# A fused attention and two-layer feed-forward kernel: zero matmuls in TensorE's waits, a new order of the work ahead of the first gate product, and another order of weight conversion

## The chip, the cores and the metric

The kernel runs on one core of a Trainium2 chip. The metric is the device time of one execution in microseconds (us): the median of the executions that were timed. A NeuronCore has a matmul engine (TensorE; PE in the profile, with its weight loads as PEld), a vector engine (VectorE; DVE), an activation engine (ScalarE; ACT), a general one (GpSimd; POOL) and a queue that issues DMAs (SyncE; SP). Each works through its own list of instructions in order; an instruction that waits holds up everything behind it on its engine.

## The reference

Windowed attention over 4 batches, 8 heads, 768 positions of 64 (chunks of 32 queries, each with 8 memory keys, 16 positions to the left and 8 to the right), then two feed-forward stages over 3072 tokens of width 512, all in float32:

```python
scores = scale * np.matmul(q_c, k_full.transpose(0, 1, 3, 2))
a = np.exp(scores - np.max(scores, axis=-1, keepdims=True))
out[:, :, c_start:c_end] = np.matmul(a / (np.sum(a, axis=-1, keepdims=True) + 1e-09), v_full)
...
gate = 1.0 / (1.0 + np.exp(-(x @ w_gate)))          # w_gate, w_val: 512 x 1536
x = gate * (x @ w_val) @ w_out                      # w_out: 1536 x 512
...
h = x @ w_in                                        # 512 x 2048
g = (a[0] + a[1]*h + a[2]*h*h + a[3]*h**3) / (1.0 + np.abs(b[0])*np.abs(h) + np.abs(b[1])*h*h + 1e-6)
return g @ w_out
```

The weights of both stages reach the chip as float64 words (8 bytes each).

## The kernel before

**Tiles.** The attention works on 24 tiles of 128 query rows (32 queries of four chunks, all eight heads). Per tile `attn_qk` makes the scores in two PSUM banks `sp` (L98), `attn_max` takes the row maximum and subtracts it on DVE (L122, L123 or, away from the ends of a sequence, L129, L131), `attn_exp` is one ACT instruction (L137), `attn_sum` and `attn_mul` normalise on DVE (L144 to L146, L150), `attn_t` transposes on TensorE (`tp`, L157) and copies on ACT (L159), and `attn_pv` multiplies with the values (`xp`, L172) and writes the result as a pair of halves: the part that the matmul format holds, by ACT (L181), and the rest, by DVE (L182). Four tiles make one block `x` of 512 tokens.

**First feed-forward stage.** Six blocks j by twelve slices f of the hidden width are 72 steps. A step runs `gate_val` twice (m = 0 gate, m = 1 value; L250), each 12 products of 128x128 by 128x512: four pieces of the inner dimension times three terms (high by high, high by low, low by high). ACT makes the sigmoid `sg` of the gate (L259), DVE multiplies it with the value product (L262), and `g_split` makes the pair `g` of it (ACT L268, then DVE L269). `out1` of a step runs one step later: 12 products that add up in four PSUM banks `acc` (L282) over a block's twelve steps. The second stage (from L331) comes after block 5.

**Weights.** Slice f has three units of weights, (f, 0) gate, (f, 1) value, (f, 2) output. In block 0 each is loaded (`load_stage`, 512 KB, tile `st`) and converted from float64: `conv_scale`, two ACT instructions (L202, L203); `conv_mag`, then `conv_sign`, one DVE instruction each (L207, L214), which leave float32 in `wf`. Before a unit is used in any block it is split into the pair `wp`: `split_hi` on ACT (L233), `split_lo` on DVE (L237). So in block 0 a unit costs three instructions on ACT and three on DVE, and they depend on each other in the order scale, mag, sign, hi, lo.

**Order.** The order on every engine is that in which the program is written. Ahead of the 72 steps stands a list written out by hand (L488 on): loads, the attention of tiles 0 to 3, and the conversion of the six units of f = 0 and 1 and the scaling of the units of f = 2. In the steps a plan says what is done in each: split of slice f+1, bits (`bits1`: mag and sign) of f+2, scaling of f+3, parts of later attention tiles:

```python
run(w1_hi, attn_exp, bits1)
gate_val(j, f, 0, c0, n)
run(w1_lo, attn_sum, attn_mul, pv, attn_t)
gate_val(j, f, 1, c0, n)
run(scale1)
g_split((1, j, f, c0), sgs.pop((j, f, c0)), n)
run(attn_qk, attn_max, conv2)
```

A PSUM bank of the pool `ps` (four banks; `acc` holds the other four) is given out again when its last reader is through.

## Time and profile before

| | |
|---|---|
| three timed executions | 1206.11, 1207.27, 1208.91 us; median 1207.27 |
| the profiled execution | 1208.78 us, of which 1207.0 us lie between the first and the last instruction (its span) |
| busy time of PE | 1185.7 us, 98% of the span |
| busy time of DVE, ACT | 891.4 us (74%), 749.2 us (62%) |
| first score product | 4.60 us after the span's start |
| first gate product | 30.84 us |
| first output product (`acc`) | 44.76 us |

The profile gives each engine's busy time, tables of busy time and granted TensorE clock by stretch, the instructions in order of time, and for each idle stretch what ended it. Matmuls overlap, so PE counts as busy while products follow each other, whatever the clock is.

### The profile page before, as it was taken

Reading aid. Unit: us, or ns where it says so; the run is one execution under the profiler, and the core shown is the slowest. Engines: PE = TensorE matmul, PEld = TensorE weight load, DVE = VectorE, ACT = ScalarE, POOL = GpSimd, SP = SyncE. Lnnn points to the kernel's source line nnn. Section 1 sums busy time; section 2 is a strip of 40 time slices with the busy share of each in tenths; the row PEclk is TensorE's granted clock in tenths of the full one; section 3 lists DMA queues with packets and bytes.
Section 4 is the critical chain, followed back from the end, with each engine's and each line's share of the span. In section 5 each row is a group of like instructions: output and inputs, shape, how many; then the busy total and the mean of one; then the engine's idle time right before and its main releaser. Section 6 shows DMA issues by size and latency. Waiting matters only on the chain.

```text
span 1207.0 us, 19977 instructions
## 1 busy us (share of the span) xinstructions
PE 1185.7 (98%) x8064; PEld 973.7 (81%) x8064; DVE 891.4 (74%) x1458; ACT 749.2 (62%) x1302; POOL 2.1 (0%) x15
## 2 busy tenths in 40 slices
...
GB/s 366 293 189 128 24 153 57 136 89 164 80 121 154 68 111 85 169 71 74 162 150 53 36 70 9 39 23 9 53 18 1 53 18 1 52 18 1 36 1 35
DMA packets 39980, 101.69 MB, mean 84 GB/s; under 512 B 4560, under 2 KB 4560, under 8 KB 39888
## 3 DMA queue, kind: packets, MB, share of 16 engines
...
q8 instruction: 63, 1.03, 0.4%
...
## 4 chain that ended last, share of the span: by engine, by line
PE 92%; DVE 3%; ACT 2%; DMA 2%; issue 0%; SPq 0%; POOL 0%; POOLq 0%; DVEq 0%
PE h L250 29%; PE acc L370 22%; PE h L331 22%; PE acc L282 15%; PE xp L172 2%; PE sp L98 1%; PE tp L157 1%; DMA st<-w_in 1%; DMA v<-v_in 1%; DVE wf L207 1%; DVE wp L237 1%; DVE wf L214 1%; ACT st L202 0%; ACT st L203 0%; ACT g L268 0%
## 5 line engine op out<-in xcount | busy, mean ns | idle before, releaser
L250 PE MATMUL h<-x,wp 128*128 128x512 f32 x1728 | 416.0, 394 | 1.3 <-DVE wp L237 0.8
L250 PEld LDWEIGHTS h<-x,wp 128*128 128x128 f32 x1728 | 324.2, 189 | 69.7 <-DVE wp L237 1.5
L331 PE MATMUL h<-x,wp 128*128 128x512 f32 x1152 | 276.5, 389 | 0.0
L370 PE MATMUL acc<-wp,g 128*128 128x512 f32 x1152 | 275.9, 389 | 0.0
L331 PEld LDWEIGHTS h<-x,wp 128*128 128x128 f32 x1152 | 216.2, 188 | 44.9
L370 PEld LDWEIGHTS acc<-wp,g 128*128 128x128 f32 x1152 | 216.2, 188 | 44.9
L282 PE MATMUL acc<-g,wp 128*128 128x512 f32 x864 | 211.0, 393 | 0.0
L282 PEld LDWEIGHTS acc<-g,wp 128*128 128x128 f32 x864 | 160.6, 188 | 35.3
L268 ACT ACTIVATE g<-sg 128x512 fp32r<-128x512 f32 x72 | 45.5, 632 | 180.7 <-DVE sg L262 180.7
L339 ACT ACTIVATE t<-h,cf 128x512 f32<-128x512 f32 x96 | 74.7, 778 | 131.1 <-PE h L331 131.1
L262 DVE TENSOR_TENSOR sg<-sg,h 128x512 f32<-128x512 f32 x72 | 49.5, 687 | 130.8 <-PE h L250 126.7
L237 DVE TENSOR_TENSOR wp<-wf,wp 128x512 fp32r<-128x512 f32 x216 | 136.2, 684 | 0.1
L233 ACT ACTIVATE wp<-wf 128x512 fp32r<-128x512 f32 x216 | 120.9, 621 | 5.9 <-DVE c L214 4.0
L342 DVE TENSOR_TENSOR t<-t,h 128x512 f32<-128x512 f32 x96 | 65.9, 686 | 47.8 <-ACT hh L341 46.4
L259 ACT ACTIVATE sg<-h 128x512 f32<-128x512 f32 x72 | 43.0, 597 | 88.8 <-PE h L250 88.7
L269 DVE TENSOR_TENSOR g<-sg,g 128x512 fp32r<-128x512 f32 x72 | 49.9, 693 | 52.1 <-ACT g L268 52.1
L343 DVE SCALAR_TENSOR_TENSOR t<-t,cf,h 128x512 f32<-128x512 f32 x96 | 71.8, 748 | 3.4
L351 ACT ACTIVATE y<-qq,qc 128x512 f32<-128x512 f32 x96 | 70.1, 730 | 3.9 <-DVE qq L344 3.3
L357 DVE SCALAR_TENSOR_TENSOR qq<-qq,y 128x512 f32<-128x512 f32 x96 | 65.8, 686 | 8.2 <-ACT y L352 8.2
L344 DVE SCALAR_TENSOR_TENSOR qq<-hh,cab,qq 128x512 f32<-128x512 f32 x96 | 71.7, 747 | 0.0
L358 DVE SCALAR_TENSOR_TENSOR t<-t,cf,y 128x512 f32<-128x512 f32 x96 | 71.6, 746 | 0.0
L359 DVE SCALAR_TENSOR_TENSOR t<-qq,t 128x512 f32<-128x512 f32 x96 | 66.5, 693 | 3.3
...
## 6 DMA issues: line engine op xcount, KB each, us to landing
...
```

The source lines that it names most:

```text
L233: nc.scalar.activation(out=wp[key][:, 0], in_=src, func=ACTF.Copy)
L237: nc.vector.tensor_tensor(out=t[:, 1], in0=src, in1=t[:, 0].bitcast(F32), op=ALU.subtract)
L250: nc.tensor.matmul(pt, lhsT=w[:, a, kt * P : (kt + 1) * P], rhs=x[:, kt, b, c0 : c0 + n], start=(kt == 0 and i == 0), stop=(kt == KT - 1 a ...
L282: nc.tensor.matmul(acc[j][d][:, c0 : c0 + n], lhsT=w[:, a, d * P : (d + 1) * P], rhs=g[:, b, 0:n], start=(f == 0 and c0 == 0 and i == 0), ...
L331: nc.tensor.matmul(hp, lhsT=w[:, a, kt * P : (kt + 1) * P], rhs=x[:, kt, b], start=(kt == 0 and i == 0), stop=(kt == KT - 1 and i == 2),)
L339: nc.scalar.activation(out=t, in_=hp, func=ACTF.Identity, scale=cf[:, 3:4], bias=cf[:, 2:3])
L343: nc.vector.scalar_tensor_tensor(out=t, in0=t, scalar=cf[:, 1:2], in1=hp, op0=ALU.add, op1=ALU.mult)
L344: nc.vector.scalar_tensor_tensor(out=qq, in0=hh, scalar=cab[:, 1:2], in1=qq, op0=ALU.mult, op1=ALU.add)
L351: nc.scalar.activation(out=y, in_=qq, func=ACTF.Abs_reciprocal_sqrt, bias=qc[:, 0:1])
L358: nc.vector.scalar_tensor_tensor(out=t, in0=t, scalar=cf[:, 0:1], in1=y, op0=ALU.add, op1=ALU.mult)
L359: nc.vector.scalar_tensor_tensor(out=t, in0=qq, scalar=2.0, in1=t, op0=ALU.subtract, op1=ALU.mult)
L370: nc.tensor.matmul(acc[j][m], lhsT=g[:, a, m * P : (m + 1) * P], rhs=w[:, b], start=(f == 0 and i == 0), stop=(f == NF2 - 1 and i == 2),)
```

## The change

1. **Zero matmuls.** A constant tile `warm_in` of zeros (one DVE memset) and one `ps` bank. `warm(n)` issues n float32 matmuls of 128x128 by 128x256 into it; nothing reads them. 15 of them stand between the attention steps ahead of the first gate product.
2. **Scores in other banks.** The first four tiles' scores go to the `acc` banks (tiles 1 and 2 to 0 and 1, tiles 0 and 3 to 2 and 3) rather than to `ps`.
3. **Tile order.** Loads and attention of the first block go by tiles 1, 0, 2, 3. `attn_pv` is cut in two, the products and the writing of `x` (`attn_x`), which the list places apart.
4. **Weights.** The units are loaded and converted in the order (0,0), (0,1), (1,0), (1,1), (0,2), (1,2). The scaling of the three units of f = 2 and their bits, and the split of (1,2), move out of the list into step 0, behind `g_split`. In all later steps `bits1` stands behind `w1_lo` and not ahead of the gate products.

```diff
-        sps = [ps(f"sp{t}_{h}")[:, 0 : 4 * KEYS].rearrange("p (r w) -> p r w", r=4) for h in range(2)]
+        if early is None:
+            sps = [ps(f"sp{t}_{h}") for h in range(2)]
+        else:
+            sps = [accp.tile([P, 512], F32, tag=f"acc{early + h}", name=f"sp{t}_{h}") for h in range(2)]
...
+    warm_in = const.tile([P, 256], F32, name="warm_in")
+    nc.vector.memset(warm_in, 0.0)
+    warm_ps = ps("warm")
+
+    def warm(n):
+        for _ in range(n):
+            nc.tensor.matmul(warm_ps[:, 0:256], lhsT=warm_in[:, 0:P], rhs=warm_in, start=True, stop=True)
+
+    def conv1(f, m):
+        conv_mag(f"1_{f}_{m}", unit1(f, m))
+        conv_sign(f"1_{f}_{m}", unit1(f, m))
+    def hi0(f, m):
+        split_hi((1, 0, f, m), unit1(f, m))
+    def lo0(f, m):
+        split_lo((1, 0, f, m), unit1(f, m))
...
+        load_qk(1)
         load_qk(0)
-        load_qk(1)
+        load_v(1)
         load_qk(2)
-        load_v(1)
         load_v(0)
         load_qk(3)
-        load_w1(0)
+        load_v(2)
+        load_stage("1_0_0", w1[:, 0, 0:512])
         load_v(3)
+        for f, m in ((0, 1), (1, 0), (1, 1), (0, 2), (1, 2), (2, 0), (2, 1), (2, 2)):
+            load_stage(f"1_{f}_{m}", w1[:, f, m * 512 : (m + 1) * 512])
...
+        warm(5)
+        attn_qk(1, 0)
...
+        attn_t(3)
+        hi0(0, 0)
+        conv_mag("1_0_1", unit1(0, 1))
+        warm(2)
+        attn_pv(3)
+        conv_sign("1_0_1", unit1(0, 1))
+        lo0(0, 0)
+        to_x(3)
+        hi0(0, 1)
+        conv_scale("1_1_0")
+        warm(2)
+        lo0(0, 1)
+        conv1(1, 0)
+        hi0(1, 0)
+        conv_scale("1_1_1")
+        conv_mag("1_1_1", unit1(1, 1))
+        lo0(1, 0)
+        conv_sign("1_1_1", unit1(1, 1))
+        hi0(1, 1)
+        conv_scale("1_0_2")
...
-            run(w1_hi, attn_exp, bits1)
+            run(w1_hi, attn_exp)
             gate_val(j, f, 0, c0, n)
-            run(w1_lo, attn_sum, attn_mul, pv, attn_t)
+            run(w1_lo)
+            if si:
+                run(bits1)
+            run(attn_sum, attn_mul, pv, attn_t)
             gate_val(j, f, 1, c0, n)
             run(scale1)
             g_split((1, j, f, c0), sgs.pop((j, f, c0)), n)
+            if not si:
+                split_hi((1, 0, 1, 2), unit1(1, 2))
+                for m in range(3):
+                    conv_scale(f"1_2_{m}")
+                split_lo((1, 0, 1, 2), unit1(1, 2))
+                run(bits1)
```

How this stands on the engines is shown at three places. In the names, `st1_f_m` is the loaded unit (f, m), `wf` its float32 form, `wp1_0_f_m` its pair in block 0, `sg0_f` and `g1_0_f` the gate of step f and its pair; the number behind the last underscore only counts buffers.

First, ACT from the last writing of `x` to the sigmoid of step 0. Before:

```order
L202 ACTIVATE st1_1_1_125<-st1_1_1_125 128x512 [waits DMAHW0_49]
L203 ACTIVATE st1_1_1_125<-st1_1_1_125 128x512
L202 ACTIVATE st1_2_2_135<-st1_2_2_135 128x512 [waits DMAHW5_49]
L203 ACTIVATE st1_2_2_135<-st1_2_2_135 128x512
L202 ACTIVATE st1_2_0_131<-st1_2_0_131 128x512 [waits DMAHW3_49]
L203 ACTIVATE st1_2_0_131<-st1_2_0_131 128x512
L202 ACTIVATE st1_2_1_133<-st1_2_1_133 128x512 [waits DMAHW4_49]
L203 ACTIVATE st1_2_1_133<-st1_2_1_133 128x512
L233 ACTIVATE wp1_0_1_0_555<-wf1_403 128x512 [waits DVE_49]
L233 ACTIVATE wp1_0_1_1_557<-wf2_535 128x512 [waits DVE_49]
L233 ACTIVATE wp1_0_1_2_559<-wf2_535 128x512
L259 ACT_TABLE_LOAD
```

And changed:

```order
L211 ACTIVATE st1_1_0_125<-st1_1_0_125 128x512 [waits DMAHW6_49]
L212 ACTIVATE st1_1_0_125<-st1_1_0_125 128x512
L242 ACTIVATE wp1_0_1_0_541<-wf1_538 128x512 [waits DVE_49]
L211 ACTIVATE st1_1_1_127<-st1_1_1_127 128x512 [waits DMAHW7_49]
L212 ACTIVATE st1_1_1_127<-st1_1_1_127 128x512
L242 ACTIVATE wp1_0_1_1_549<-wf2_545 128x512 [waits DVE_49]
L211 ACTIVATE st1_0_2_129<-st1_0_2_129 128x512 [waits DMAHW0_49]
L212 ACTIVATE st1_0_2_129<-st1_0_2_129 128x512
L242 ACTIVATE wp1_0_0_2_556<-wf1_538 128x512 [waits DVE_49]
L211 ACTIVATE st1_1_2_131<-st1_1_2_131 128x512 [waits DMAHW1_49]
L212 ACTIVATE st1_1_2_131<-st1_1_2_131 128x512
L268 ACT_TABLE_LOAD
```

Four scalings and then three splits in a row have become an alternation of one split and one scaling, where each split waits for DVE.

Second, DVE in the same place, up to the last bits of these units. Before:

```order
L207 SCALAR_TENSOR_TENSOR wf2_535<-st1_1_1_125 128x512 [waits DMAHW0_49,Activation_49]
L207 SCALAR_TENSOR_TENSOR wf2_535<-st1_1_2_127 128x512 [waits DMAHW1_49]
L237 TENSOR_TENSOR wp1_0_0_2_489<-wf1_403,wp1_0_0_2_489 128x512
L214 SCALAR_TENSOR_TENSOR wf2_535<-st1_1_2_127,wf2_535 128x512 [waits DVE_49]
L214 SCALAR_TENSOR_TENSOR wf2_535<-st1_1_1_125,wf2_535 128x512
L207 SCALAR_TENSOR_TENSOR wf3_561<-st1_2_0_131 128x512 [waits DMAHW3_49,Activation_49]
L207 SCALAR_TENSOR_TENSOR wf3_561<-st1_2_1_133 128x512 [waits DMAHW4_49,Activation_49]
L207 SCALAR_TENSOR_TENSOR wf4_564<-st1_2_2_135 128x512 [waits DMAHW5_49]
L214 SCALAR_TENSOR_TENSOR wf3_561<-st1_2_0_131,wf3_561 128x512 [waits DVE_49]
L214 SCALAR_TENSOR_TENSOR wf3_561<-st1_2_1_133,wf3_561 128x512 [waits DVE_49]
L214 SCALAR_TENSOR_TENSOR wf4_564<-st1_2_2_135,wf4_564 128x512 [waits DVE_49]
```

And changed:

```order
L216 SCALAR_TENSOR_TENSOR wf1_538<-st1_1_0_125 128x512 [waits DMAHW6_49,Activation_49]
L223 SCALAR_TENSOR_TENSOR wf1_538<-st1_1_0_125,wf1_538 128x512 [waits DVE_49]
L216 SCALAR_TENSOR_TENSOR wf2_545<-st1_1_1_127 128x512 [waits DMAHW7_49,Activation_49]
L246 TENSOR_TENSOR wp1_0_1_0_541<-wf1_538,wp1_0_1_0_541 128x512 [waits DVE_49]
L223 SCALAR_TENSOR_TENSOR wf2_545<-st1_1_1_127,wf2_545 128x512 [waits DVE_49]
L216 SCALAR_TENSOR_TENSOR wf1_538<-st1_0_2_129 128x512 [waits DMAHW0_49,Activation_49]
L246 TENSOR_TENSOR wp1_0_1_1_549<-wf2_545,wp1_0_1_1_549 128x512 [waits DVE_49]
L223 SCALAR_TENSOR_TENSOR wf1_538<-st1_0_2_129,wf1_538 128x512 [waits DVE_49]
L216 SCALAR_TENSOR_TENSOR wf2_545<-st1_1_2_131 128x512 [waits DMAHW1_49,Activation_49]
L246 TENSOR_TENSOR wp1_0_0_2_556<-wf1_538,wp1_0_0_2_556 128x512 [waits DVE_49]
L223 SCALAR_TENSOR_TENSOR wf2_545<-st1_1_2_131,wf2_545 128x512 [waits DVE_49]
```

Two or three instructions of a kind followed each other; now each `mag` (L216) waits for ACT's scaling of its own unit, and the bits of f = 2 are no longer here.

Third, DVE from the low half of the first `g` on. Before:

```order
L269 TENSOR_TENSOR g1_0_0_0_607<-sg0_0_0_582,g1_0_0_0_607 128x512 [waits Activation_49]
L207 SCALAR_TENSOR_TENSOR wf4_564<-st1_3_0_545 128x512 [waits DMAHW6_49]
L207 SCALAR_TENSOR_TENSOR wf5_627<-st1_3_1_547 128x512 [waits DMAHW7_49]
L207 SCALAR_TENSOR_TENSOR wf5_627<-st1_3_2_549 128x512 [waits DMAHW0_49]
L214 SCALAR_TENSOR_TENSOR wf4_564<-st1_3_0_545,wf4_564 128x512 [waits DVE_49]
L214 SCALAR_TENSOR_TENSOR wf5_627<-st1_3_1_547,wf5_627 128x512 [waits DVE_49]
L214 SCALAR_TENSOR_TENSOR wf5_627<-st1_3_2_549,wf5_627 128x512 [waits DVE_49]
L237 TENSOR_TENSOR wp1_0_2_0_620<-wf3_561,wp1_0_2_0_620 128x512 [waits Activation_49]
L237 TENSOR_TENSOR wp1_0_2_1_622<-wf3_561,wp1_0_2_1_622 128x512 [waits DMAHW2_49,Activation_49]
L237 TENSOR_TENSOR wp1_0_2_2_624<-wf4_564,wp1_0_2_2_624 128x512 [waits Activation_49]
L262 TENSOR_TENSOR sg0_1_0_646<-sg0_1_0_646,h0_1_1_0_651 128x512 [waits PE_49,Activation_49]
```

And changed:

```order
L278 TENSOR_TENSOR g1_0_0_0_608<-sg0_0_0_586,g1_0_0_0_608 128x512 [waits Activation_49]
L246 TENSOR_TENSOR wp1_0_1_2_611<-wf2_545,wp1_0_1_2_611 128x512 [waits Activation_49]
L216 SCALAR_TENSOR_TENSOR wf3_620<-st1_2_0_133 128x512 [waits DMAHW2_49,Activation_49]
L216 SCALAR_TENSOR_TENSOR wf3_620<-st1_2_1_135 128x512 [waits DMAHW3_49,Activation_49]
L216 SCALAR_TENSOR_TENSOR wf4_623<-st1_2_2_137 128x512 [waits DMAHW4_49,Activation_49]
L223 SCALAR_TENSOR_TENSOR wf3_620<-st1_2_0_133,wf3_620 128x512 [waits DVE_49]
L223 SCALAR_TENSOR_TENSOR wf3_620<-st1_2_1_135,wf3_620 128x512 [waits DVE_49]
L223 SCALAR_TENSOR_TENSOR wf4_623<-st1_2_2_137,wf4_623 128x512 [waits DVE_49]
L246 TENSOR_TENSOR wp1_0_2_0_638<-wf3_620,wp1_0_2_0_638 128x512 [waits Activation_49]
L246 TENSOR_TENSOR wp1_0_2_1_640<-wf3_620,wp1_0_2_1_640 128x512 [waits Activation_49]
L246 TENSOR_TENSOR wp1_0_2_2_642<-wf4_623,wp1_0_2_2_642 128x512 [waits Activation_49]
L216 SCALAR_TENSOR_TENSOR wf4_623<-st1_3_0_563 128x512 [waits DMAHW6_49]
```

Between the low half of `g` of step 0 and the low splits of f = 2 (`wp1_0_2_m`) stood the bits of f = 3; now the low split of (1,2) and the bits of f = 2 stand there, and the bits of f = 3 come after those splits.

## Rows read from the trace of the kernel before

**Rows 1.** The page, busy time (share of the span) and instructions of each engine.

```profile
PE 1185.7 (98%) x8064; PEld 973.7 (81%) x8064; DVE 891.4 (74%) x1458; ACT 749.2 (62%) x1302; POOL 2.1 (0%) x15
```

**Rows 2.** Stretches: length, busy us (instructions) by engine, granted clock, DMA share, GB/s.

```profile
17.50:21.00 3.50, 2.08 (x71) 1.71 (x71) 3.36 (x9) 3.50 (x8) 0.00 (x0) 1.00 1.04 402
21.00:34.60 13.60, 10.68 (x205) 8.92 (x204) 10.94 (x22) 10.82 (x25) 0.00 (x0) 0.50 1.03 405
34.60:99.50 64.90, 62.58 (x574) 50.20 (x573) 57.99 (x102) 52.97 (x95) 0.34 (x2) 1.00 0.66 229
99.50:103.00 3.50, 3.50 (x10) 2.69 (x9) 3.50 (x7) 3.50 (x8) 0.00 (x0) 0.51 0.45 112
```

**Rows 3.** PE in order of time: start, us, line, tiles, count [idle before, releaser].

```profile
4.60 1.17 PE L98 MATMUL sp<-k,q 64*32 64x64 f32 x64 [4.60 <-DMA k<-k_in]
...
17.83 1.14 PE L172 MATMUL xp<-at,v 64*64 64x32 f32 x64 [0.28 <-ACT at L159]
...
22.08 2.41 PE L172 MATMUL xp<-at,v 64*64 64x32 f32 x64 [0.43 <-ACT at L159]
...
30.84 7.97 PE L250 MATMUL h<-x,wp 128*128 128x512 f32 x26 [0.48 <-ACT x L181]
...
39.60 5.32 PE L250 MATMUL h<-x,wp 128*128 128x512 f32 x22 [0.79 <-DVE wp L237]
44.76 2.88 PE L282 MATMUL acc<-g,wp 128*128 128x512 f32 x12
47.48 5.74 PE L250 MATMUL h<-x,wp 128*128 128x512 f32 x24
...
97.75 1.13 PE L172 MATMUL xp<-at,v 64*64 64x32 f32 x62 [1.53 <-DVE s L131]
...
99.22 4.59 PE L250 MATMUL h<-x,wp 128*128 128x512 f32 x12
```

**Rows 4.** Waits of DVE from 37 to 100 us: total us, times, longest.

```profile
DVE g L269 <- ACT g L268: 6.4, 7, 1.6
```

**Rows 5.** Waits of DVE from 5 to 35 us.

```profile
DVE x L182 <- ACT x L181: 1.9, 2, 1.4
DVE r L144 <- ACT s L137: 1.0, 2, 0.8
DVE m L129 <- PE sp L98: 0.8, 1, 0.8
```

**Rows 6.** DVE in order of time.

```profile
9.95 0.70 DVE L129 TENSOR_REDUCE m<-sp 128x4 f32<-128x256 f32 x2
10.57 0.74 DVE L131 TENSOR_TENSOR s<-sp,m 128x256 f32<-128x256 f32 x2
11.24 0.74 DVE L129 TENSOR_REDUCE m<-sp 128x4 f32<-128x256 f32 x2
...
12.56 0.67 DVE L144 TENSOR_REDUCE r<-s 128x8 f32<-128x512 f32 x1
...
13.60 1.24 DVE L150 TENSOR_TENSOR s<-s,r 128x512 f32<-128x512 f32 x2
...
43.58 1.89 DVE L207 SCALAR_TENSOR_TENSOR wf<-st 128x512 int32<-128x512 int32 x3
...
47.20 1.89 DVE L237 TENSOR_TENSOR wp<-wf,wp 128x512 fp32r<-128x512 f32 x3
```

**Rows 7.** ACT in order of time.

```profile
15.55 0.67 ACT L202 ACTIVATE st<-st 128x512 f32<-128x512 f32 x1 [3.56 <-DMA st<-w_in]
...
37.21 1.28 ACT L259 ACT_TABLE_LOAD   x1
...
38.99 0.66 ACT L202 ACTIVATE st<-st 128x512 f32<-128x512 f32 x1
...
42.32 0.62 ACT L268 ACTIVATE g<-sg 128x512 fp32r<-128x512 f32 x1
42.84 1.66 ACT L233 ACTIVATE wp<-wf 128x512 fp32r<-128x512 f32 x3
```

More of the change, by code (lines that the diff above doesn't have):

```diff
@@ L159, in attn_t, with attn_pv @@
         nc.scalar.activation(out=at, in_=tp, func=ACTF.Copy)
-    def attn_pv(t, x, n0):
+    xp_ps = {}
+    def attn_pv(t):
         vt, at = vs.pop(t), at_sb.pop(t).rearrange("p (r q) -> p r q", r=4)
-        xps = [ps(f"xp{t}_{h}")[:, 0:256].rearrange("p (k n) -> p k n", k=2) for h in range(2)]
+        xps = xp_ps[t] = [ps(f"xp{t}_{h}")[:, 0:256].rearrange("p (k n) -> p k n", k=2) for h in range(2)]
         for k in range(2):
@@ L178, in attn_pv, with attn_x @@
                         )
-        for h in range(2):
+    def attn_x(t, x, n0):
+        for h, xps in enumerate(xp_ps.pop(t)):
             hi, lo = (x[:, 2 * h : 2 * h + 2, b, n0 : n0 + P] for b in range(2))
-            nc.scalar.activation(out=hi, in_=xps[h], func=ACTF.Copy)
-            nc.vector.tensor_tensor(out=lo, in0=xps[h], in1=hi.bitcast(F32), op=ALU.subtract)
+            nc.scalar.activation(out=hi, in_=xps, func=ACTF.Copy)
+            nc.vector.tensor_tensor(out=lo, in0=xps, in1=hi.bitcast(F32), op=ALU.subtract)
     stage = {}
@@ L222, in unit1 @@
         u = 3 * f + m
-        if u % 2 == 0 and u // 2 not in wf:
+        if u // 2 not in wf:
             wf[u // 2] = wpool.tile([P, 2, 512], F32, tag="w", name=f"wf{u // 2}")
@@ L387, in fused_kernel, with to_x @@
     NB1 = len(BLOCKS1)
-    def pv(t):
-        j, n0 = t // 4, t % 4 * P
-        if n0 == 0:
-            xt[j] = xpool.tile([P, KT, 2, 512], F32R, tag="x", name=f"x{j}")
-        attn_pv(t, xt[j], n0)
+    def to_x(t):
+        j = t // 4
+        if j not in xt:
+            xt[j] = xpool.tile([P, KT, 2, 512], F32R, tag="x", name=f"x{j}")
+        attn_x(t, xt[j], t % 4 * P)
+    def pv(t):
+        attn_pv(t)
+        to_x(t)
+    warm_in = const.tile([P, 256], F32, name="warm_in")
[11 more added lines that the diff above has]
+        split_lo((1, 0, f, m), unit1(f, m))
     def scale1(f):
```

87 lines of the change are left out of this document (39 added, 48 removed).

## The prediction, made before the changed kernel ran

> **What bounds the kernel now.** I read the page's busy times first: PE 98% [rows 1]. So the time is PE's work plus what PE lost, and the loss sits at the start. The table by stretches shows the clock: 1.00 from 17.5 to 21 us, 0.50 (1.2 of 2.4 GHz) to 34.6, full again, once more 0.51 from 99.5 to 103 [rows 2]. PE in order of time shows the rest [rows 3]: the first gate product starts at 30.84, the 60 products of steps 0 and 1 end at 47.48. That is 16.64 us; 12 products at full clock take 2.72 (44.76 to 47.48), 60 take 13.6, so 3.0 us went to the half clock and a wait of 0.79. Afterwards PE waits visibly only at 97.75, 1.53 us for DVE, and the clock dips behind it.
>
> The view that decides is another: whom does **DVE** wait for? From 37 to 100 us for one thing alone, the high half of `g` from ACT, 6.4 us in 7 times [rows 4]. This is built into each step (multiply, ACT's high half, low half). It never waits there for a product of PE, although PE shows 98%. In block 0 every step has nine conversion instructions on DVE, 9 x 0.60 = 5.4 us (three take 1.89, so they start 0.60 apart [rows 6]), besides the gate and later attention tiles, against 3 x 2.72 = 8.2 us of products. DVE is a second bound through block 0, as close as PE, and PE's wait at 97.75 shows that no lead is left by then. Whatever DVE is late, PE is late at that place.
>
> **The change, part by part.** *Loads.* DMA runs at 402 to 405 GB/s up to 34.6 us [rows 2]. Tile 1 takes tile 0's place, so the first scores still come at 4.6. Unit (0,0) moves behind v2: its ACT instruction waited for the load until 15.55 [rows 7]; 0.5 MB more at 0.4 MB per us make about 16.9, and ACT hides the 1.3, as this scaling now stands behind the copy of the third tile's transposes. Later units land 1.3 us apart and are wanted 3.7 apart (below): no cost. The scores in `acc` banks cost nothing: these are free until the first output product. The memset runs while DVE has nothing to do before 5.8.
>
> *Zero matmuls.* 15 of 256 columns in float32, a form that isn't in the trace. Lower bound: half of a 512-column gate product, 0.11 each, 1.7 us in all; upper: two records each, as the scores have (64 for 32 products [rows 3]), at twice the columns' time and half clock, 0.9 each, 13.6 us. Most lie in PE's waits; on the path are those right ahead of the transposes and the value products, 0.3 to 2 us. I take 0.5, near the lower end, since most of them lie where PE idles. What they can give back: 64 records of value products take 1.14 at full and 2.41 at half clock [rows 3], 1.2 us per tile.
>
> *Attention until the last bits of unit (1,0).* This instant, T, is the end of a long run on DVE. It starts at 4.60 + 1.17 = 5.8 when the first scores are done [rows 3]. Tiles 1, 2, 3 take 0.62 + 0.67 (reduce, subtract) + 1.04 (sum to multiply) + 0.62 = 2.95 each [rows 6], tile 0 about 3.1, four pairs for `x` 0.67 each (two 128x256 operations, like the subtract), the bits of three units 1.3 each, two low splits 0.6: 8.9 + 3.1 + 2.7 + 3.9 + 1.2 = 19.8. So T is 25.6 with no wait at all. The trace of before has 1.9 + 1.0 + 0.8 = 3.7 us of waits of these kinds in the same stretch [rows 5]; the dependences stay, hence 29.3. Half clock on the value products delays each `x` by up to 1.2: upper end 29.3 + 4.8 = 34.1. I take T = 30.5, one tile's worth, since the zero matmuls should save some but before had only 3.5 us of full clock in that time.
>
> *The alternation.* Here is the cost. From T on ACT does the high split of (1,0), then scales (1,1): 0.03 + 0.53 (three splits 1.66 [rows 7]) + 0.56 + 0.67 = 1.8. Only then can DVE form the bits of (1,1), with the low split of (1,0) between: 0.6 + 0.6 + 0.69 = 1.9. One round is 3.7 us, and in each both engines idle for half. Rounds follow for (1,1), (0,2) and (1,2). ACT is through with its scaling of (1,2) at T + 7.4 + 1.7 = T + 9.1. Behind it in ACT's list stands the sigmoid of step 0, whose product was done long before: table and sigmoid 1.78 (37.21 to 38.99), six scalings of f = 3, 3.33 (38.99 to 42.32), high half of `g`, 0.62 [rows 7]: the first output product can start at **T + 14.8** = 45.3, not earlier than the 44.76 of before, though the gates begin some 3 us earlier (26 to 29). PE meanwhile does 48 products and then waits about 5 us.
>
> Then ACT has the split of (1,2) and six scalings of f = 2, which before were done ahead of step 0: T + 18.7. DVE makes the last `mag` (0.6) and three signs (1.8): the low splits of f = 2 start at **T + 21.1** = 51.6, against 47.20 [rows 6], 4.4 us late. Moreover, the bits of f = 3 were done by then and are now still to come: 6 x 0.60 = 3.6. DVE is 8.0 us behind, with nothing in later steps that saves DVE work. Moving `bits1` behind `w1_lo` in the later steps only exchanges neighbours on DVE.
>
> *Sum.* PE gives this back nowhere: at step 2 it waits for those splits (4 us late), at the value products of tile 4 (97.75) for DVE. From there PE bounds and the lag stays: +8.0 on the profiled execution's 1208.8 makes 1216.8. That execution lay 1.5 above the median of the three, so **1215.3** by the median. With T from 25.6 to 34.1 the lag is 3.1 to 11.6: 1210.4 to 1218.9.
>
> *A rule against the change.* After PE's wait up to 97.75 the clock was at 0.51 from 99.5 to 103, and 12 gate products took 4.59 [rows 2, 3]. The Trainium skill (TensorE: Matmul & The Clock Gate, "HAM oscillation — how this bites in real kernels") has it that each burst of matmuls behind a wait starts at the lower clock again; no zero matmul stands in the wait ahead of the first output product. By that rule these 12 would take 5.4 in place of 2.7; the trace agrees with the rule at 97.75. In my sum it costs nothing, as the next gate comes 5.8 behind them anyway (T + 20.6).
>
> **The rivals.**
>
> A, faster: PE keeps the early start. Gates at about 27 and no half clock under them would save 30.84 - 27 + 3.0 = 6.8, 1200.5. It needs DVE to have slack in block 0. For it: 98% PE, and DVE's mean of 74% [rows 1]. Against it: rows 4, where DVE never waits for PE. It turns on the alternation being under 2 us per round. 9%.
>
> B, no change: T near 25.6, and PE without the wait and dip at 97.75 (1.5 + 1.7), so that a lag of 3.1 is made up: about 1207. For it: DVE could wait less than before, as all loads come in order of use. Against it: the same waits on ACT are in the list, and a late DVE makes the wait at 97.75 likelier. 10%.
>
> C, slower still: the zero matmuls don't hold the clock, so T is at 34.1, and the clock stays half into step 2 after PE's long wait, 1.9 for a second stretch as before the 34.6 one: 1218.9 + 1.9 = 1220.8. For it: before, the clock fell at 21 although PE was busy 2.08 of the last 3.5 us [rows 2]. Against it: zero matmuls fill part of the waits that there were before. 11%.
>
> **How the numbers follow.** My forecast has 70%: 1215.3, from 1210.4 to 1218.9; C 11%, B 10%, A 9%. The range of 8 in 10 reaches a little over its ends, into B's and C's sides: 1209.5 to 1219.5. What measurement can tell from no change is about 0.2%, 2.4 us (1204.9 to 1209.7): faster 0.09, same 0.10, slower 0.81.
>
> **What would show it.** In the changed profile: the first gate product at 26 to 29 us; ACT's high splits of (1,0), (1,1), (0,2) about 3.7 us apart, each released by DVE, and DVE's L216 waiting for ACT some 1.9 us three times; a wait of PE of about 5 us ahead of the first output product (L291), released by ACT's `g`, which starts at 43 to 47; the first low split of f = 2 at about 51.6; a second wait of PE there; the clock at half behind these waits. I am wrong if the rounds take 2 us, if the gate of step 2 starts at 45 or earlier, or if DVE shows waits for PE in block 0.

## The result, and the profile after

The changed kernel takes **1220.09 us** (median of 4, 1219.10 to 1221.65) against 1208.09 of the kernel before in the same session (4, 1206.11 to 1209.11): ratio 1.0102 with a 95% interval of 1.0084 to 1.0121, 12.0 us slower. The prediction had the direction and most of the mechanism (+8.0 us, at most 1219.5), and the time lies just above its range.

The page, busy time of each engine of the changed kernel, as in [rows 1]; PE is as full as before:

```profile
PE 1194.7 (98%) x8094; PEld 978.0 (80%) x8094; DVE 893.0 (73%) x1459; ACT 749.1 (62%) x1302; POOL 2.1 (0%) x15
```

Stretches of the changed kernel, columns as in [rows 2]:

```profile
12.50:17.50 5.00, 3.50 (x165) 2.72 (x154) 4.54 (x13) 2.16 (x5) 0.00 (x0) 1.00 1.02 408
17.50:20.40 2.90, 0.07 (x4) 0.10 (x6) 2.18 (x6) 0.63 (x1) 0.00 (x0) 0.95 1.04 408
20.00:30.20 10.20, 9.17 (x166) 7.54 (x166) 5.85 (x13) 5.13 (x11) 0.00 (x0) 0.51 1.02 403
30.20:47.50 17.30, 13.44 (x104) 10.29 (x100) 9.80 (x16) 10.93 (x20) 0.00 (x0) 0.99 0.69 270
47.50:54.20 6.70, 4.45 (x10) 3.24 (x11) 3.20 (x5) 6.15 (x12) 0.00 (x0) 0.50 0.00 0
```

PE of the changed kernel in order of time, as in [rows 3] (L415 are the zero matmuls, L103 scores, L179 value products, L259 gate and value, L291 output):

```profile
1.19 4.63 PE L415 MATMUL warm<-warm_in 128*128 128x256 f32 x10 [1.19 <-DVE warm_in L409]
5.76 1.06 PE L103 MATMUL sp<-k,q 64*32 64x64 f32 x64
...
13.98 1.06 PE L179 MATMUL xp<-at,v 64*64 64x32 f32 x57 [0.90 <-issue]
...
20.33 1.93 PE L179 MATMUL xp<-at,v 64*64 64x32 f32 x64 [3.04 <-DMA st<-w_in]
...
26.51 0.44 PE L179 MATMUL xp<-at,v 64*64 64x32 f32 x8 [0.70 <-issue]
...
31.78 9.30 PE L259 MATMUL h<-x,wp 128*128 128x512 f32 x38
41.71 2.56 PE L259 MATMUL h<-x,wp 128*128 128x512 f32 x10 [0.63 <-DVE wp L246]
49.75 5.27 PE L291 MATMUL acc<-g,wp 128*128 128x512 f32 x12 [5.48 <-ACT g L277]
55.69 0.73 PE L259 MATMUL h<-x,wp 128*128 128x512 f32 x2 [0.68 <-ACT wp L242]
...
110.26 1.13 PE L179 MATMUL xp<-at,v 64*64 64x32 f32 x62 [2.18 <-DVE s L136]
...
111.73 3.01 PE L259 MATMUL h<-x,wp 128*128 128x512 f32 x12
```

The gates don't start earlier (31.78 against 30.84), the first output product comes 5.0 us later, and tile 4's value products, at 97.75 in [rows 3], come at 110.26: 12.5 us late, and again waiting for DVE. Three waits of PE (0.90, 3.04, 0.70) stand inside or just ahead of the value products; of them below.

DVE of the changed kernel in order of time, as in [rows 6] (L216 mag, L223 sign, L246 low split):

```profile
22.72 0.76 DVE L191 TENSOR_TENSOR x<-xp,x 128x256 fp32r<-128x256 f32 x2 [2.93 <-ACT x L190]
...
34.18 0.69 DVE L223 SCALAR_TENSOR_TENSOR wf<-st,wf 128x512 int32<-128x512 int32 x1
36.68 0.69 DVE L216 SCALAR_TENSOR_TENSOR wf<-st 128x512 int32<-128x512 int32 x1 [1.80 <-ACT st L212]
...
40.36 0.69 DVE L216 SCALAR_TENSOR_TENSOR wf<-st 128x512 int32<-128x512 int32 x1 [1.79 <-ACT st L212]
...
44.05 0.69 DVE L216 SCALAR_TENSOR_TENSOR wf<-st 128x512 int32<-128x512 int32 x1 [1.79 <-ACT st L212]
...
56.10 1.89 DVE L246 TENSOR_TENSOR wp<-wf,wp 128x512 fp32r<-128x512 f32 x3
...
59.71 1.89 DVE L223 SCALAR_TENSOR_TENSOR wf<-st,wf 128x512 int32<-128x512 int32 x3
```

ACT of the changed kernel, as in [rows 7] (L242 high split, released by DVE's sign):

```profile
34.91 0.63 ACT L242 ACTIVATE wp<-wf 128x512 fp32r<-128x512 f32 x1 [1.49 <-DVE wf L223]
...
38.61 0.63 ACT L242 ACTIVATE wp<-wf 128x512 fp32r<-128x512 f32 x1 [1.96 <-DVE wf L223]
...
42.29 0.63 ACT L242 ACTIVATE wp<-wf 128x512 fp32r<-128x512 f32 x1 [1.96 <-DVE wf L223]
...
49.07 0.62 ACT L277 ACTIVATE g<-sg 128x512 fp32r<-128x512 f32 x1
```

Unit (1,0) has its bits at 34.18 + 0.69 = 34.87: this is T, forecast at 30.5. From there everything is where the prediction puts it: high splits 3.7 apart, first output product at T + 14.9, low splits of slice 2 at T + 21.2.

One number, chosen with the runs in hand, serves for all that follows. **E** is the instant at which DVE is through with both the low splits of slice 2 and the bits of slice 3. Before, the bits come first and the splits end at 47.20 + 1.89 = 49.09 [rows 6]; after, the bits come last and end at 59.71 + 1.89 = 61.60. E is 12.5 late, and the time 12.0.

### The profile page after: what moved, and what is told of

Same layout as the page of the kernel before. It is cut to its first block, busy times and chain, and to the rows that moved or that the text cites. A ratio compares the mean times of both kernels' runs of the same rounds, so it can differ in the third digit from the quotient of the medians.

```text
span 1217.3 us, 20055 instructions
## 1 busy us (share of the span) xinstructions
PE 1194.7 (98%) x8094; PEld 978.0 (80%) x8094; DVE 893.0 (73%) x1459; ACT 749.1 (62%) x1302; POOL 2.1 (0%) x15
## 4 chain that ended last, share of the span: by engine, by line
PE 92%; DVE 3%; ACT 3%; DMA 1%; issue 1%; SPq 0%; POOL 0%; DVEq 0%; POOLq 0%
PE h L259 29%; PE acc L379 21%; PE h L340 21%; PE acc L291 15%; PE xp L179 2%; PE sp L103 1%; PE tp L162 1%; DVE wf L223 1%; DVE wf L216 1%; DMA v<-v_in 1%; DMA st<-w_in 1%; ACT st L212 1%; ACT st L211 1%; DVE wp L246 1%; ACT wp L242 0%
## 5 line engine op out<-in xcount | busy, mean ns | idle before, releaser
L259 PE MATMUL h<-x,wp 128*128 128x512 f32 x1728 | 413.6, 392 | 3.0 <-DVE wp L246 1.0
L259 PEld LDWEIGHTS h<-x,wp 128*128 128x128 f32 x1728 | 321.6, 188 | 72.0 <-DVE wp L246 2.3
L291 PE MATMUL acc<-g,wp 128*128 128x512 f32 x864 | 213.1, 395 | 5.6 <-ACT g L277 5.5
L291 PEld LDWEIGHTS acc<-g,wp 128*128 128x128 f32 x864 | 161.9, 189 | 41.9 <-ACT g L277 5.9
L246 DVE TENSOR_TENSOR wp<-wf,wp 128x512 fp32r<-128x512 f32 x216 | 136.3, 684 | 0.1
L242 ACT ACTIVATE wp<-wf 128x512 fp32r<-128x512 f32 x216 | 121.4, 621 | 12.7 <-DVE wf L223 6.8
```

Of the source, the lines that this page charges most:

```text
L242: nc.scalar.activation(out=wp[key][:, 0], in_=src, func=ACTF.Copy)
L246: nc.vector.tensor_tensor(out=t[:, 1], in0=src, in1=t[:, 0].bitcast(F32), op=ALU.subtract)
L259: nc.tensor.matmul(pt, lhsT=w[:, a, kt * P : (kt + 1) * P], rhs=x[:, kt, b, c0 : c0 + n], start=(kt == 0 and i == 0), stop=(kt == KT - 1 a ...
L291: nc.tensor.matmul(acc[j][d][:, c0 : c0 + n], lhsT=w[:, a, d * P : (d + 1) * P], rhs=g[:, b, 0:n], start=(f == 0 and c0 == 0 and i == 0), ...
```

## Experiments

Each kernel's time is compared with the runs of the kernel before on the same chip in the same session (1208.34 for e1 to e4, 1207.90 for e5 to e8, 1207.38 for e9 to e12); a bare difference to the changed kernel's 1220.09 leaves out that the sessions differ by up to 1 us.

**e1: no zero matmuls.** All 15 are left out, with their tile, its memset and their bank.

```diff
-        for _ in range(n):
-            nc.tensor.matmul(warm_ps[:, 0:256], lhsT=warm_in[:, 0:P], rhs=warm_in, start=True, stop=True)
+        pass
```

> The changed kernel without its 15 zero matmuls. Theory 1 (the order of conversion makes the lag, and PE's late instructions set T): the last bits of unit (1,0) at T of about 34 in place of 34.87, first output product about 49.1 instead of 49.75, time 0 to 1.5 us below the changed kernel, about 1219. The stalls inside value products stay at the same counts of matmul records (about 221, 348 and 474 from the first), which are now other instructions, since 18 to 30 records are missing: in the middle of the value products of tiles 1, 0 and at the start of tile 3's. Theory 2 (the zero matmuls themselves cost the unforeseen 4 us, by delaying scores and transposes): T near 30.5, first output product near 45, 1215 to 1216. Theory 3 (they are the whole loss): back to about 1208.

1219.83 us (1218.88 to 1222.84), ratio 1.0095 (1.0078 to 1.0111). Whatever they cost and give together is too small to tell. T is 35.10 (sign at 34.41). PE of e1 in order of time:

```profile
12.36 0.95 PE L179 MATMUL xp<-at,v 64*64 64x32 f32 x25
14.57 1.29 PE L179 MATMUL xp<-at,v 64*64 64x32 f32 x39 [1.25 <-issue]
...
18.70 0.53 PE L179 MATMUL xp<-at,v 64*64 64x32 f32 x19 [0.69 <-ACT at L164]
21.87 1.50 PE L179 MATMUL xp<-at,v 64*64 64x32 f32 x45 [2.63 <-issue]
```

This gave the main clue. In the changed kernel the first wait stands behind 7 value products of tile 1, the second ahead of tile 0's. In e1, with 18 and 20 records of zero matmuls fewer ahead of them, both have moved into the middle of a tile, behind 25 and 19 of a tile's 64 records, where data or a bank is no likely cause. Counted from PE's first matmul, the first stands behind record 221 in both kernels, the second behind 348 and 347; the third wait of the changed kernel stands behind 474. The waits belong to a place in PE's instruction list, some 126 matmul records apart, not to the instruction that stands there. The label "DMA st<-w_in" at 20.33 only names what happened to end last.

**e2: no alternation.** Every scaling stands one place earlier, so that DVE has the next unit to work on.

```diff
         conv1(1, 0)
-        hi0(1, 0)
         conv_scale("1_1_1")
+        hi0(1, 0)
         conv_mag("1_1_1", unit1(1, 1))
+        conv_scale("1_0_2")
         lo0(1, 0)
...
-        conv_scale("1_0_2")
         conv_mag("1_0_2", unit1(0, 2))
+        conv_scale("1_1_2")
...
-        conv_scale("1_1_2")
```

> The changed kernel with each unit's scaling one place earlier in the list, ahead of the split of the unit before it, so that ACT never holds a scaling behind a split that waits for DVE. Theory 1: T unchanged at about 35; three rounds of 3.7 us shrink to about 2.1 each, the first output product comes at about 45.2 instead of 49.75, the first low split of f = 2 at about 51.7 instead of 56.10; time 4 to 5 us below the changed kernel, about 1215.5. Theory 2 (the alternation is hidden behind something else, loads or PE): no change, 1220.

1216.78 us (1216.30 to 1217.91), ratio 1.0073 (1.0058 to 1.0088): 3.3 faster than the changed kernel. DVE of e2: the rounds take 2.0 us and no L216 waits (T 34.56).

```profile
34.47 0.69 DVE L216 SCALAR_TENSOR_TENSOR wf<-st 128x512 int32<-128x512 int32 x1
...
36.47 0.69 DVE L216 SCALAR_TENSOR_TENSOR wf<-st 128x512 int32<-128x512 int32 x1
...
38.46 0.69 DVE L216 SCALAR_TENSOR_TENSOR wf<-st 128x512 int32<-128x512 int32 x1
...
51.27 1.89 DVE L246 TENSOR_TENSOR wp<-wf,wp 128x512 fp32r<-128x512 f32 x3
```

The low splits of slice 2 come 4.83 earlier; E is 56.77. So the alternation is real and costs 3 to 5 us, but not most of the loss.

**e3: weights not loaded.** GpSimd fills the units instead (slices 0 to 5), to free the DMA engines.

```diff
-        nc.sync.dma_start(out=stage[key], in_=src)
+        if key[0] == "1" and int(key.split("_")[1]) < 6:
+            nc.gpsimd.memset(stage[key].bitcast(F32), 1.0)
+        else:
+            nc.sync.dma_start(out=stage[key], in_=src)
```

> The changed kernel, but the stage-one weights of slices 0 to 5 are not loaded: POOL fills those tiles with a constant, so that no weight load competes with anything after the attention loads, which end near 14 us. Instruction packets and data share the DMA engines. Theory 1 (PE ran out of instructions because their packets queue behind saturated loads): the waits of PE of 3.04 and 0.70 us at matmul records 348 and 474 are gone or under 0.5, the value products of tile 0 start at about 18 instead of 20.33, T is 30 to 32 instead of 34.87, first output product 45 to 48. Theory 2 (that wait of 3 us is one for a PSUM bank, a reader or the value load): it stays at about 3 us, T stays near 35.

1219.92 us (one run), T 34.84: no verdict on either theory. PE's waits on issue were gone, but PE also came to those places late, as the fills had held DVE up. GpSimd and DVE of e3:

```profile
9.79 2.73 POOL L203 MEMSET st<- 128x1024 f32 x3
```

```profile
9.79 2.75 DVE L150 TENSOR_SCALAR r<-r 128x8 f32<-128x8 f32 x1
```

An operation on 8 columns, 0.17 us elsewhere, lasted as long as three fills, and PE then waited 3.82 for tile 1's normalised scores. The experiment brought in a cost of its own; e5 takes that out.

**e4: DVE's wait filled, in the kernel before.** The sign of unit (f+2, 2) is taken out of `bits1` and stands between the two halves of `g`.

```diff
         nc.scalar.activation(out=t[:, 0, 0:n], in_=sg, func=ACTF.Copy)
+        between()
         nc.vector.tensor_tensor(out=t[:, 1, 0:n], in0=sg, in1=t[:, 0, 0:n].bitcast(F32), op=ALU.subtract)
...
-        for m in range(3):
+        for m in range(2):
             conv_sign(f"1_{f}_{m}", unit1(f, m))
+
+    def bits_last(f):
+        conv_sign(f"1_{f}_2", unit1(f, 2))
...
```

> The kernel before, with one thing moved in block 0: the sign bits of the third unit of each slice stand between ACT's high half and DVE's low half of the gate pair, where DVE waited 0.7 to 1.6 us in every step; nothing is added or left out. Theory 1 (DVE bounds block 0 and each us that it loses is lost at the end): DVE gains about 0.6 us in each of eight to ten steps, the wait of PE at 97.75 and the clock dip behind it vanish, block 1 starts 4 to 5 us earlier, time about 1203. Theory 2 (PE bounds block 0 with 98% busy, DVE's place is slack): within 1 us of before, 1207 to 1208.

1204.94 us (1204.71 to 1206.01), ratio 0.9974 (0.9964 to 0.9983). DVE's waits from 37 to 100 us, as in [rows 4], and the stretch from 34.6:

```profile
DVE g L270 <- ACT g L268: 3.2, 3, 1.7
```

```profile
34.60:100.00 65.40, 65.40 (x583) 52.87 (x582) 61.36 (x107) 55.68 (x101) 0.34 (x2) 1.00 0.66 229
```

PE is busy without a gap, and the wait at 97.75 [rows 3] is gone. DVE's list, not PE's, set block 0, as the prediction's first part says; 3.2 us less waiting there gave 3.4, less than the 5 that I had expected. The clock does not explain it: the stretch from 21.0 to 34.6 ran at a granted 1.00 in this execution and at 0.50 in that of the kernel before [rows 2], with the same list on PE, yet the gates started later here, at 31.84 against 30.84.

**e5: weights not loaded, without the clash.** As e3, but the units of slices 3 to 5 are filled only after tile 3's split.

```diff
+        if after is not None:
+            nc.gpsimd.tensor_copy(out=stage[key].bitcast(F32)[:, 0:1], in_=after)
...
+            late = xt[0][:, 0, 0, 384:385].bitcast(F32) if f == 3 and m == 0 else None
-            load_stage(f"1_{f}_{m}", w1[:, f, m * 512 : (m + 1) * 512])
+            load_stage(f"1_{f}_{m}", w1[:, f, m * 512 : (m + 1) * 512], late)
...
```

> The changed kernel without the loads of the stage-one weights of slices 0 to 5: GpSimd fills slices 0 to 2 with ones in the first 10 us, and the later ones only after tile 3's split, so that no fill runs beside VectorE's small operations on the sums (in e3 one of these took 2.75 us at 9.79, under three fills, where it takes 0.17). The output is not the reference's. Theory (TensorE's value products wait for their instructions, which come late while loads fill the DMA engines): no wait of TensorE marked issue or put down to a load before the gates, T (end of the sign of unit (1,0)) at 31 to 32.5 instead of 34.9, the first output product at T + 14.9, and about 1216.5 to 1218 us. Rival (T is late by the order of the work itself): T at 34 or later, about 1220 us.

1217.63 us (one run), T 32.01 + 0.69 = 32.70. PE of e5, and its stretches:

```profile
13.55 1.06 PE L179 MATMUL xp<-at,v 64*64 64x32 f32 x57 [0.98 <-issue]
...
20.07 1.14 PE L179 MATMUL xp<-at,v 64*64 64x32 f32 x64 [2.01 <-DMA q<-q_in]
...
22.52 1.94 PE L179 MATMUL xp<-at,v 64*64 64x32 f32 x64
...
29.60 6.77 PE L265 MATMUL h<-x,wp 128*128 128x512 f32 x27
```

```profile
12.50:17.50 5.00, 3.63 (x134) 3.15 (x127) 4.90 (x14) 1.43 (x4) 0.00 (x0) 0.74 0.99 363
17.50:20.40 2.90, 0.89 (x25) 0.36 (x25) 1.76 (x5) 0.86 (x2) 0.00 (x0) 0.86 0.27 86
20.00:25.00 5.00, 4.93 (x137) 4.21 (x138) 3.20 (x8) 2.78 (x7) 0.00 (x0) 0.67 0.30 88
```

I had expected no wait at all; two stayed. But queries, keys and values alone still moved 363 GB/s up to 17.5. The wait of 2.01, from 18.06 on, stands where the DMA engines had little to do (86 GB/s from 17.5 to 20.4); the part on late instructions below says what it was for. Behind that, at 88 GB/s, the third wait, inside tile 2's 64 products, is gone. T lies just above the 31 to 32.5 that the theory of late instructions gave, 2.2 earlier than in the changed kernel, and the gates start 2.2 earlier.

**e6: weight loads held.** Nothing is left out; the loads only start later, behind a one-column copy by GpSimd that reads tile 1's (then tile 2's) result.

```diff
+        if after is not None:
+            nc.gpsimd.tensor_copy(out=stage[key].bitcast(F32)[:, 0:1], in_=after)
         nc.sync.dma_start(out=stage[key], in_=src)
...
         to_x(1)
+        for i, (f, m) in enumerate(((0, 0), (0, 1), (1, 0), (1, 1), (0, 2), (1, 2))):
+            load_stage(f"1_{f}_{m}", w1[:, f, m * 512 : (m + 1) * 512], None if i else xt[0][:, 0, 0, 128:129].bitcast(F32))
...
```

> The changed kernel with all its loads, but those of the weights of slices 0 and 1 start only when tile 1's values are split (about 15 to 16 us), and the rest when tile 2's are: the DMA engines are free of weights when TensorE reaches the 221st and 348th matmul record. Theory (late instructions): the wait of 3.0 us ahead of tile 0's value products shrinks to under 1 us, T at 32 to 33.5, 2 to 3 us faster than the changed kernel, 1217 to 1218. Rival (the waits are for data, or belong to the order): the waits stay, the weights come later, T at 35 or later, 1220 to 1222.

1218.01 us (1216.74 to 1219.55), ratio 1.0086 (1.0071 to 1.0101): 2.1 faster than the changed kernel (1.9 with the sessions taken into account), though every weight of slices 0 to 2 comes later. PE of e6, and two stretches:

```profile
14.02 1.06 PE L179 MATMUL xp<-at,v 64*64 64x32 f32 x57 [0.92 <-issue]
...
18.01 1.14 PE L179 MATMUL xp<-at,v 64*64 64x32 f32 x64 [0.74 <-DVE s L136]
...
24.38 0.44 PE L179 MATMUL xp<-at,v 64*64 64x32 f32 x8 [1.07 <-issue]
```

```profile
12.50:17.50 5.00, 3.51 (x165) 2.74 (x158) 4.51 (x13) 2.19 (x5) 0.57 (x1) 1.00 0.70 238
...
20.00:25.00 5.00, 3.93 (x71) 3.16 (x72) 3.52 (x8) 1.86 (x4) 0.00 (x0) 0.52 1.03 415
```

Where the loads had paused (238 GB/s) the wait of 3.04 is 0.74; where they run again (415 GB/s) one of 1.07 stands at the old place. T is 33.23, 1.6 earlier. The waits follow what the DMA engines have to move.

**e7: DVE's wait filled, in the changed kernel.** e4's edit on the changed kernel.

```diff
-            g_split((1, j, f, c0), sgs.pop((j, f, c0)), n)
+            g_split((1, j, f, c0), sgs.pop((j, f, c0)), n, lambda: run(bits_last) if si else None)
...
```

> The changed kernel with e4's edit: the sign of the third unit stands between the two splits of the gated values, so that VectorE works while it waits for ScalarE. T and the rounds of 3.7 us stay as they are (T at 34.9, first output product at 49.8). Theory (VectorE bounds block 0 behind the late start): the gain is that of e4 or a little more, 3 to 4 us, 1216 to 1217. Rival (after the change TensorE or ScalarE bounds block 0): under 1 us, 1219.5 to 1220.

1217.30 us (1216.47 to 1217.51), ratio 1.0078 (1.0061 to 1.0095): 2.8 faster (2.6 with the sessions taken into account), a little less than expected; DVE's wait for `g` is 4.4 us instead of 7.2. It holds for the changed kernel too that VectorE bounds block 0.

**e8: as e4, the loads of slice 2 held** until tile 1's values are split (25 us).

```diff
-        load_w1(2)
...
         pv(1)
+        for m in range(3):
+            load_stage(f"1_2_{m}", w1[:, 2, m * 512 : (m + 1) * 512], None if m else xt[0][:, 0, 0, 128:129].bitcast(F32))
         pv(2)
```

> The kernel before with e4's edit, and the loads of the weights of slice 2 and later start only when tile 1's values are split (about 25 us) instead of at once, so that the DMA engines are idle when TensorE asks for the instructions behind record 473. Theory (late instructions): the wait of 1.9 us marked issue in tile 3's value products (29.65 in e4) goes, the gates start at about 30 instead of 31.84, 1203 to 1204 against e4's 1204.94. Rival (that wait is not for instructions): it stays, 1205 or more.

1204.91 us (1204.31 to 1205.98), as e4. PE of e8:

```profile
24.68 3.64 PE L172 MATMUL xp<-at,v 64*64 64x32 f32 x128 [0.18 <-DMA v<-v_in]
29.79 6.58 PE L252 MATMUL h<-x,wp 128*128 128x512 f32 x18 [1.48 <-ACT x L181]
...
39.64 5.30 PE L252 MATMUL h<-x,wp 128*128 128x512 f32 x22 [1.46 <-DVE wp L239]
```

The wait inside tile 3's products (1.92 in e4) is gone and the gates start 2.05 earlier than in e4, as the theory has it; the time is no shorter. ACT waits 1.86 for the load of the unit that it scales first, which I had put last among the three, and PE loses 1.46 at 39.64.

**e9: the changed attention start, the units in about the old order.** The list's attention part stays; units go (0,0), (0,1), (0,2), (1,0), ... and the plan of the steps is that of before.

```diff
+        conv_scale("1_0_0")
         warm(1)
         attn_pv(0)
+        conv_mag("1_0_0", unit1(0, 0))
+        conv_scale("1_0_1")
+        conv_sign("1_0_0", unit1(0, 0))
         to_x(0)
...
-            run(w1_hi, attn_exp)
+            run(w1_hi, attn_exp, bits1)
             gate_val(j, f, 0, c0, n)
-            run(w1_lo)
-            if si:
-                run(bits1)
...
```

> The changed kernel's attention start (zero matmuls, scores in the output sums' banks, tile 1 first) with the weight units in about the order of the kernel before: all three units of slice 0 first, the bits of slice 1's third unit and the scaling of slice 2 ahead of the gates, the main loop as it was before. Theory (the loss lies in the new order of the weight units: the late start of unit (1,0) and the rounds, which VectorE can't make up in block 0): low splits of slice 2 begin at 48 to 50, and 1208.5 to 1211 us. Rival (the loss lies in the attention start, in TensorE's waits and the later gates): 1215 us or more.

1209.61 us (1208.23 to 1210.44), ratio 1.0014 (1.0005 to 1.0024). PE still waits 0.72, 2.80 and 0.83 in the value products and the gates still start at 31.50, but the loss is 2.2 instead of 12. The attention start (zero matmuls, banks, tile order, with the waits that it brings) loses little by itself; its parts were not separated, and the converse, the new order of units behind the old attention start, was not run. In e9 DVE has units to convert while the values are late (its waits for `x` up to 35 us are 1.7 against 4.5).

**e10: e2, and slice 2 where it was.**

```diff
+        for m in range(3):
+            conv_scale(f"1_2_{m}")
         for si, (j, f, c0, n) in enumerate(steps):
...
             run(w1_hi, attn_exp)
+            if not si:
+                run(bits1)
             gate_val(j, f, 0, c0, n)
...
-                for m in range(3):
-                    conv_scale(f"1_2_{m}")
...
```

> e2 (each unit's scaling one place earlier), and slice 2 is scaled and its bits are made where the kernel before does it: scaling ahead of the gates, bits ahead of the output product. The units of slices 0 and 1 keep the changed order. Theory (each piece of the order costs VectorE waits that add up): another 2 to 3 us on e2's 1216.78, so 1213.5 to 1215. Rival (slice 2's place is free, T alone decides): as e2, 1216 to 1217.5.

1213.98 us (1213.21 to 1216.00), ratio 1.0053 (1.0038 to 1.0068): another 2.8 by the medians, 1.8 when e2 and e10 are each taken against the kernel before of their session. E is 53.62 + 1.89 = 55.51.

**e11: e10 with e6's held loads and e7's filled wait.**

```diff
...
+            g_split((1, j, f, c0), sgs.pop((j, f, c0)), n, lambda: run(bits_last))
...
```

> e10 with e6's held weight loads and e7's filled wait. If the terms add (3.3 of e2, 2 to 3 of slice 2, 2.1 of e6, 2.8 of e7): 1209 to 1210.5 us. If they overlap, because VectorE no longer bounds block 0 once some of them are in: 1211 to 1213. Either way above e4's 1204.94, since unit (1,0) stays late.

1209.64 us (1208.52 to 1210.38), ratio 1.0016 (1.0006 to 1.0025). The four terms add up: 3.3 + 2.8 + 2.1 + 2.8 = 11.0 off 1220.1 makes 1209.1. Taken against the kernel before of each session they are 3.6 + 1.8 + 1.9 + 2.6 = 9.9 off the 12.0, which leaves 2.1; measured are 2.3.

**e12: e8 with the third unit's load first.**

```diff
-        for m in range(3):
+        for m in (2, 0, 1):
```

> e8, with the held loads of slice 2 in the order in which ScalarE scales them, the third unit first (in e8 ScalarE waited 1.86 us for it at 31.1, and TensorE later 1.5 us for a low split). Theory (in e4 and e8 TensorE has no wait left in block 0, so the gates' start at 29.8 instead of 31.84 counts once no load is late): TensorE's wait for the low split goes, 1203 to 1204. Rival (VectorE's sum in block 0 sets the end whatever the start): as e4 and e8, 1204.5 to 1205.5.

1204.07 us (1203.86 to 1204.35), ratio 0.9969 (0.9956 to 0.9981): faster than either kernel. PE of e12, and its stretch from the gates on:

```profile
30.05 13.43 PE L252 MATMUL h<-x,wp 128*128 128x512 f32 x48 [1.51 <-ACT x L181]
43.32 2.88 PE L285 MATMUL acc<-g,wp 128*128 128x512 f32 x12
```

```profile
30.05:99.50 69.45, 69.45 (x595) 55.42 (x596) 65.17 (x115) 60.12 (x108) 0.34 (x2) 1.00 0.75 270
```

48 products in a row without a wait, and none for 69 us. Tile 4's value products come at 94.53, in e8 at 96.08 and in e4 at 96.61, and the three spans are 1202.2, 1203.1 and 1204.2: in the profiled executions the earlier gates now count. By medians against the kernel before the gain is 3.3, 3.0 and 3.4, and the intervals overlap: that e12 beats e4 isn't shown.

## Why the prediction was right, and where it was wrong

**DVE as the second bound: right.** It carries the whole case. E of each kernel that keeps DVE's order in the steps (start of the last three bits or splits, plus their 1.89), and how late it and the time are against the kernel before (E minus 49.09; median minus that of before in the same session):

| kernel | E, us | E later | time later |
|---|---|---|---|
| changed | 59.71 + 1.89 = 61.60 | 12.5 | 12.0 |
| e1 no zero matmuls | 59.88 + 1.89 = 61.77 | 12.7 | 11.5 |
| e3 weights not loaded, fills beside DVE | 59.66 + 1.89 = 61.55 | 12.5 | 11.6 |
| e6 weight loads held | 58.04 + 1.89 = 59.93 | 10.8 | 10.1 |
| e5 weights not loaded | 57.53 + 1.89 = 59.42 | 10.3 | 9.7 |
| e2 no alternation | 54.88 + 1.89 = 56.77 | 7.7 | 8.4 |
| e10 and slice 2 as before | 53.62 + 1.89 = 55.51 | 6.4 | 6.6 |
| e9 units in old order | 49.19 + 1.89 = 51.08 | 2.0 | 2.2 |

The time follows E within 1.2 us, in eight kernels whose gates start between 29.6 and 32.7. When TensorE's gates start does not show in it. E is read in one execution and the time is a median; by the spans of those same executions the two agree within 2.2 (changed kernel: E 12.5, span 10.3 later).

**The failed step is the term T**: "I take T = 30.5", with 34.1 as its upper end. It was 34.87, and 4.4 later is what the forecast lacked: 8.0 + 4.4 = 12.4 against 12.0. Its own pieces, from the trace: first scores done at 6.87 instead of 5.8 (+1.1: the first five zero matmuls run to 5.82; in e1, without them, the scores start at 4.92); DVE busy 20.5 instead of 19.8 (+0.7); waits of 6.9 instead of 4.9 (+2.0; 4.5 of them for `x`); gaps between instructions +0.7. The first isn't a cause by itself, since e1 without it has T at 35.10. The waits for `x` are. I had priced them by [rows 5], "the dependences stay", and bounded them by half clock on the value products. No row I had chosen prices a PE that stands still in the middle of a tile, and the trace of before had one, PE in order of time:

```profile
28.64 1.72 PE L172 MATMUL xp<-at,v 64*64 64x32 f32 x55 [1.65 <-issue]
```

It stands behind record 473, the place of the changed kernel's third wait, and taking it away gained nothing (e8): DVE had units to convert there. The change did two things at once. It drew the attention's work up to the places where PE's list runs dry while loads fill the DMA engines (e5, e6), and it took the conversions out of DVE's list there, which had covered such waits (e9). So the step that failed is the term of waits in T: it priced the waits of before once more and put those of PE for its own instructions at nothing. Holding the loads gives back 1.6 of T, not loading the weights 2.2; this settles half of the 4.4. The other half, the waits left in e5 behind loads of the attention itself, and gaps, wasn't separated further.

**Late instructions** are shown by their places, by their cause, and in the traces themselves. The places are fixed by count (e1). The waits go with the DMA load (e5, e6, e8). The profile's DMA view lists a queue of kind "instruction" with 5 packets, 0.08 MB in the first 45 us of the changed kernel, 16 KB each; its page has for the whole execution:

```profile
q8 instruction: 63, 1.03, 0.3%
```

The Trainium skill (Runtime: NRT & Kernel Launch, "Instruction fetch mechanics") says that engines take their instructions in blocks of 16 KiB, 256 each, by a DMA of their own, and calls the cost mostly hidden. The places agree: 126 matmul records and as many weight loads are some 252 instructions, and 63 blocks of 256 are the 8064 matmuls and 8064 weight loads of the kernel before [rows 1]. "Mostly hidden" doesn't hold here: 3.04 us for one block in the changed kernel and up to 3.18 (e10), at 400 GB/s.

The times of these packets in the traces settle it. In the changed kernel they are through at 12.64, 18.68 and 24.98, and the waits end at 13.98, 20.33 and 26.51. In the fourteen traces together 26 waits of 0.6 us and more stand behind records 221, 347 or 348, and 473 or 474, and each ends 1.3 to 1.7 us after such a packet; where PE passes one of these places without a wait, the packet had been through for at least 1.5 us. What the last 1.3 to 1.7 us are for isn't shown. What the loads delay is the packet: it starts 3.6 to 4.9 us after the wait before it has ended while loads run at some 400 GB/s, 1.4 us after it in e6 (238 GB/s), and 1.1 us after it in e5 at 21.15, where the DMA engines had been idle. The wait of 2.01 in e5 is of this kind too: its packet started only at 17.36, behind the loads of queries, keys and values, and was through at 18.44.

**Alternation: right.** Rounds of 3.7 (L216 waits 1.80, 1.79, 1.79 for ACT; I had 1.9), first output product at T + 14.9 (said 14.8), low splits at T + 21.2 (said 21.1). e2 puts 3.3 us on it (3.6 with the sessions taken into account) and e10 2.8 (1.8) on slice 2's place.

**Zero matmuls: right by the net.** I bounded all 15 together by 1.7 and 13.6 and put 0.5 of that on the path. A lone one takes 0.60 with its two records, one in a pair 0.57 (1.13 for four records at full clock), or 0.96 (1.91) at half; e1 finds no difference. What they were to give back, full clock over the value products, they gave in part at most: the granted clock was 0.51 from 20.0 to 30.2 all the same, behind PE's 3.04 us without work. From 30.2 to 35.2 it was full, where e1 had 0.50; but e4 and the kernel before differ as much with the same list on PE (e4, above), so that it is their doing isn't shown, and the time shows nothing of it.

**Loads: half right.** No unit was waited for, as I said. That their traffic costs PE its instructions I didn't see: 2.1 us (e6).

**The gates at 26 to 29: wrong**, 31.78; PE's three waits ahead of them are 4.6 us together. It had no weight in the sum, as the prediction's own argument has it, and e9 shows it again.

**The rule on the clock: agrees in part.** Behind the wait of 5.48 the 12 output products took 5.27 (the text gave 5.4), at a granted 0.50 from 47.5 to 54.2, and it cost nothing: the next gate waited for ACT and DVE until 56.84. One thing went the other way: behind the wait at 110.26 the clock did not fall, 12 gate products took 3.01 against 4.59 in [rows 3]. This gives back 1.6 us in the two profiled executions, which differ by 10.3 (1219.10 against 1208.78). It is a matter of the execution: behind the same wait of 2.18 at 110.47 in e1 the clock was 0.50 from 110.5 to 117.0 and the 12 gate products took 4.86.

**Rivals.** A and B fell: rounds took 3.7, T was late. C's number (1220.8) is the nearest, and its T of 34.1 nearly right; its reason is not shown: the clock was indeed at half over the value products from 20.0 to 30.2, but T is the same without zero matmuls (e1), it is 34.56 in e2, whose clock was at 0.83 in that stretch, and the half clock into step 2 was hidden. A range whose upper end takes T's bound for the bound of the whole had no room for a cause that isn't in the rows. That the median still lies within 1 us of the range's end is luck in part: that margin was meant for half clock.
